# Two batches of chunk 1 transposed by DMA, and chunk 2's first attention products moved into the next stage

## The chip, the cores and the metric

The kernel runs on one core of a Trainium2 chip. The metric is the time of one execution in microseconds (us), as the device measures it; the median of several runs counts. The profiles are those of single executions. Engines are named as in the profile: PE is TensorE (PEld its weight loads), DVE is VectorE, ACT is ScalarE, POOL is GpSimd, SP is SyncE, which only issues DMAs here.

## The reference

Retention (a linear attention with decay), then a feed-forward layer with a tanh GELU. The inputs q, k, v have 4 batches, 8 heads, 768 steps and 64 dimensions; x has 3072 tokens of 512.

```python
gamma = 1.0 - 2.0 ** (-5.0 - np.arange(H))
for t in range(S):
    state = gamma[None, :, None, None] * state + np.einsum('bhd,bhe->bhde', k[:, :, t], v[:, :, t])
    y[:, :, t] = scale * np.einsum('bhd,bhde->bhe', q[:, :, t], state)
x = y.transpose(0, 2, 1, 3).reshape(B * S, H * D)
h = x @ w_in                  # 512 -> 2048
g = 0.5 * h * (1.0 + np.tanh(c * (h + 0.044715 * h * h * h)))
out = g @ w_out               # 2048 -> 512
```

Everything is given and returned in float32.

## The kernel before

**Chunks and stages.** The 768 steps are cut into 6 chunks of 128. A chunk has all 4 batches, so 512 tokens. For each chunk `c` and batch `b` the attention is done in parts: q and k are cast to f16 (`prep1`, on ACT from chunk 1 on; they lie together in a tile `qk`), v is scaled by decays and cast (`prep1` on POOL); q and k are transposed into `qkT`; `mm_A` makes the products of k and q within the chunk on PE, in two PSUM banks of the tag "att" (it has four), and `ev_A` masks them into `a_sb` on DVE; `mm_yc` (what the state from earlier chunks gives) and `mm_yi` (what this chunk gives) are added up in one bank, which `ev_Y` turns into the f16 activations `xT` on DVE; `mm_s` and `ev_S` bring the state `st` up to date. Heads go in pairs, `NHP` = 4.

**Transposes.** There are two ways. `mm_T` and `ev_T` (chunks 0 and 1): 8 PE transposes of a batch into an "att" bank and a copy out of it on DVE or ACT. `dma_T` (from chunk 2 on): one DMA transpose from `qk` to `qkT`, issued on SP's queue, where it waits for the casts of q and k.

**Feed-forward.** M1 of a chunk: `x @ w_in` into "h" banks (two of them), then GELU on ACT into `g`. For chunk 1 M1 has 16 units of 8 matmuls of 256 tokens (`moe1_two`): units 0 to 7 take batches 0 and 1, units 8 to 15 batches 2 and 3. W of a chunk (the change's own words call it M2): `g @ w_out` by a scheme with 7 products instead of 8, each over 8 row pairs `fp` and two halves `a` of tokens, in the banks "o" (two of them). It uses sums of `g` (`g_sums`, results `s_g[1]` to `s_g[4]`, four operations in the order 1 to 4; on POOL for chunk 1, in four calls) and sums of the weights. `units_w(c)` gives W as 14 units, product by product, two halves each: units 0 and 1 take product 0, units 2 and 3 product 1, units 4 and 5 product 2, which reads `s_g[2]`, and so on. Products 0, 2 and 3 are followed by copies on ACT (`s_p`, `s_u`, `s_q`), the others by additions on DVE, and two stores of a chunk go out on POOL's queue. W of chunk 0 is its own list of 15 units (`units_0`, lines 520 to 607), with copies `s_p` (after unit 6), `s_u` (after unit 8) and `s_q` (after unit 9), in which the last product P4 makes units 13 and 14.

**What sets the order.** The schedule is written out by hand. `run(units, after)` calls the units in turn and, after unit `i`, the functions listed in `after[i]`. Each engine carries out its instructions in just this order, and waits where an operand isn't ready or a buffer isn't free. The same goes for SP's queue: a load or a `dma_T` that waits holds up all that stand behind it. The 'ld' buffers hold two chunks of q, k and v in f32.

**Around the change.** The list at line 742 runs W of chunk 0 with chunk 1's attention in between: `preps(1, b)` casts q and k on ACT and v on POOL, `att_T(b)` transposes, `att_1A(b)` is `mm_A` and `ev_A`, `mm_Y` is `mm_yc` and `mm_yi`. The list at line 761 runs M1 of chunk 1; here the rest of chunk 1's attention stands (batches 2 and 3), the casts and transposes of chunk 2 (`prep_qk(2, b)` after units 6, 8, 10 and 12), and after unit 14 the first `mm_A` of chunk 2, of batches 0 and 1, by `att_AY`. The list at line 783 runs W of chunk 1, with chunk 2's attention: `att_AY(2, (0, 1), "h", 2, (2, 3), AC)` makes y of batches 0 and 1 and `mm_A` of batches 2 and 3. The loads of chunk 1 stand on SP at lines 728 to 730, all those of chunk 2 at once behind them (line 731), those of chunk 3 after `prep_qk(2, 3)`.

Of the kernel before, what the change touches and what calls it, by code (L numbers as in the profile page):

```python
# [16 lines left out]
def kernel(  # L17
# [10 lines left out]
    B, H, S, Dh = q.shape  # L28
# [31 lines left out]
    att = ctx.enter_context(tc.tile_pool(name="att", bufs=4))  # L60
# [23 lines left out]
    def load1(eng, nm, c, b):  # L84
        eng.dma_start(
            out=ld_tile(nm, c, b),
            in_=srcs[nm][b, :, c * C:(c + 1) * C, :].rearrange("h p d -> p h d"),
        )
# [60 lines left out]
    def prep1(eng, nm, c, b):  # L149
        if nm == "v":  # L150
            t = pre.tile([128, H, Dh], F16, tag="v16", bufs=2 * B, name="v16")
        else:
            if (c, b) not in qk16:
                qk16[c, b] = pre.tile([128, 2, H, Dh], F16, tag="qk16", bufs=2 * B, name="qk16")
            t = qk16[c, b][:, "qk".index(nm)]
        src = ld_tile(nm, c, b)
        if (nm == "v") == (c < 1):
            copy_on(eng, t, src)
        else:
            col = OQ if nm == "q" else OK  # L160
            eng.tensor_tensor(  # L161
                out=t,
                in0=src,
                in1=cst[:, col:col + H].unsqueeze(2).broadcast_to([128, H, Dh]),
                op=ALU.mult,
            )
        h16[nm, c, b] = t
# [30 lines left out]
    def dma_T(c, b):  # L198

        nc.sync.dma_start_transpose(  # L200
            out=qkT_tile(c, b).rearrange("p i hp t -> p (i hp) t"),
            in_=qk16.pop((c, b)).rearrange("p i h d -> p (i h d)"),
        )
# [411 lines left out]
    VE, AC, PO, SY = nc.vector, nc.scalar, nc.gpsimd, nc.sync  # L615
# [91 lines left out]
    def prep_qk(c, b):  # L707
        prep1(AC, "q", c, b)
        prep1(AC, "k", c, b)
        if c > 1:  # L710
            dma_T(c, b)

    def preps(c, b):
        prep_qk(c, b)
        prep1(PO, "v", c, b)
# [5 lines left out]
    def loads(c, *what):  # L721
        for nm, b in what:
            load1(SY, nm, c, int(b))
# [4 lines left out]
    loads(1, "q0", "k0", "q1", "k1", "v0", "q2", "k2", "v1", "q3", "k3")  # L728
    load_dec()
    loads(1, "v2", "v3")  # L730
    for nm in ("qk", "v"):
        loads(2, *[x + str(b) for b in range(B) for x in nm])

    def att_1A(b):
        mm_A(1, b)
# [2 lines left out]
    def mm_Y(b, tag):  # L738
# [6 lines left out]
            0: [(w_sums, 2), (g_sums, VE, 0, 6, 8)],  # L745
            1: [(w_sums, 3)],
            3: [(preps, 1, 0)],
            5: [(att_T, 0), (preps, 1, 1)],
            7: [(att_1A, 0)],
            8: [(att_T, 1)],  # L750
            9: [(preps, 1, 2)],
            10: [(att_1A, 1)],
            11: [(mm_Y, 0, "h"), (att_T, 2, AC), (ev_Y, 1, 0)],
            12: [(mm_Y, 1, "att"), (ev_Y, 1, 1), (mm_s, 1, (0,)), (preps, 1, 3)],
            13: [(att_1A, 2), (ev_S, 1, (0,))],
            14: [(att_S, 1, 1)],
        },
    )


    run(
# [3 lines left out]
            for fp in range(NF // 2)  # L765
        ],
        {
            0: [(att_T, 3)],
            1: [(mm_Y, 2, "o"), (ev_Y, 1, 2)],
            2: [(att_1A, 3)],  # L770
            3: [(att_S, 1, 2), (g_sums, PO, 1, 0, 4, 0, 1)],
            5: [(mm_Y, 3, "o"), (ev_Y, 1, 3)],
            6: [(att_S, 1, 3), (prep_qk, 2, 0)],
            7: [(g_sums, PO, 1, 4, 8, 0, 1)],
            8: [(prep_qk, 2, 1)],
            10: [(prep_qk, 2, 2)],
            11: [(g_sums, PO, 1, 0, 4, 1, 2)],
            12: [(prep_qk, 2, 3), (load, 3)],
            14: [(att_AY, 1, (), "o", 2, (0, 1), None), (prep1, PO, "v", 2, 0), (prep1, PO, "v", 2, 1)],
            15: [(g_sums, PO, 1, 4, 8, 1, 2), (prep1, PO, "v", 2, 2), (prep1, PO, "v", 2, 3)],  # L780
        },
    )
    run(
        units_w(1),
        {
            4: [(att_AY, 2, (0, 1), "h", 2, (2, 3), AC)],
            6: [(prep_qk, 3, 0)],
            7: [(att_S, 2, 0, 1)],
            8: [(prep_qk, 3, 1)],
            9: [(att_AY, 2, (2, 3), "h", 2, (), AC), (att_S, 2, 2, 3)],  # L790
            10: [(prep1, PO, "v", 3, b) for b in range(B)],
            11: [(prep_qk, 3, 2)],
            13: [(prep_qk, 3, 3)],
        },
# [54 lines left out]
```

## Time and profile before

| | |
|---|---|
| Time of 6 runs, median | 208.9 us (208.4 to 209.17) |
| Time of the profiled execution | 209.07 us |
| Its span, first to last instruction | 207.3 us |
| PE busy | 197.8 us, 95% of the span |
| ACT, POOL, DVE busy | 102.2, 111.3 and 91.5 us |
| W of chunk 0 on PE | from 34.2 to 51.4 us |
| M1 of chunk 1 on PE | from 51.4 to 70.2 us |
| W of chunk 1 on PE | from 70.2 to 86.2 us |

The busy time of an engine is a share of the whole span; how close an engine is to being the limit is read from single stretches. The chain is the work that ended last, followed back from the end from each instruction to what released it. In the views of groups and in the timeline a line gives the start, the length, the engine, the line of the code, the operation, what it writes and reads, and in brackets how long the engine had been idle and what ended that. A line can be that of a helper: line 145 is every copy or cast on ACT through `copy_on`, line 390 every sum through `tt`, line 459 the matmuls of W from chunk 1 on, line 351 those of M1, line 210 is `mm_A`, line 190 `mm_T`, line 200 `dma_T`, line 85 every load. "SPq" is SP's queue; the length of a DMA there is the time for which it holds up the queue, not the time to its landing.

### The profile page before, as it was taken

To read this page: it belongs to the slowest core of one execution; us is meant where nothing else is said; L and a number is where in the kernel's file an instruction comes from. 1 tells how busy PE (TensorE), PEld (TensorE's weight loads), DVE (VectorE), ACT (ScalarE), POOL (GpSimd) and SP (SyncE) were. 2 spreads that over 40 slices of the span, in tenths; PEclk is the share of its full clock that TensorE was granted. 3 is DMA by queue.
4 is the path that set the end of the run, shared out by engine and by line. 5 is a ranking of instruction groups with operands and counts; after the bars stand their busy time and mean duration, and the time that the engine had idled before them with its cause. 6 is when DMAs were issued, how large, how long until landed. Compare 5 with 4: busy or idle time off the path is not lost.

```text
span 207.3 us, 4685 instructions
## 1 busy us (share of the span) xinstructions
PE 197.8 (95%) x1948; PEld 136.0 (66%) x1948; DVE 91.5 (44%) x198; ACT 102.2 (49%) x181; POOL 111.3 (54%) x112
## 2 busy tenths in 40 slices
PE   5789999999999999999999999999999999999993
PEld 1447746877787888644688744678644788544882
DVE  3436389578740448400466400366301374144421
ACT  2365565545369517366445266545366411466321
POOL 0578000225188999549998259997269980200000
PEclk9999999999999999999999999999999999999999
DMA  7999999999989799999990999442520000400005
GB/s 166 288 242 217 206 206 218 255 251 222 323 207 211 177 254 233 215 256 250 268 194 23 216 328 261 90 104 47 164 96 0 2 3 5 202 0 0 3 9 193
DMA packets 98613, 34.23 MB, mean 165 GB/s; under 512 B 92320, under 2 KB 96800, under 8 KB 98592
## 3 DMA queue, kind: packets, MB, share of 16 engines
q1 hardware_dynamic: 86400, 22.40, 49.7%
q0 software_dynamic: 5664, 9.44, 19.0%
q10 hardware_dynamic: 6528, 2.10, 4.0%
q8 instruction: 15, 0.25, 0.5%
q14 instruction: 6, 0.05, 0.1%
HBM read 27.63 MB, written 6.29 MB: 164 GB/s over the span
## 4 chain that ended last, share of the span: by engine, by line
PE 89%; ACT 6%; DMA 2%; POOL 1%; issue 0%; SPq 0%; DVE 0%; POOLq 0%
PE h_ps L351 37%; PE o_ps L459 30%; PE a_ps L210 4%; PE y_ps L247 3%; PE o_ps L530 3%; PE y_ps L234 3%; PE o_ps L563 3%; ACT g L367 2%; PE qkT_ps L190 2%; DMA k<-in_k_dram 2%; ACT qk L145 2%; PE spin_ps L121 2%; PE s_ps L271 2%; ACT qkT L145 1%; POOL qk L161 1%
## 5 line engine op out<-in xcount | busy, mean ns | idle before, releaser
L351 PE MATMUL h_ps<-xT,w_in 128*128 128x512 f16 (+2 forms) x488 | 87.6, 334 | 1.4 <-ACT g L367 1.1
L367 ACT ACTIVATE g<-h_ps 128x512 f16<-128x512 f32 (+1 forms) x98 | 57.1, 588 | 31.9 <-PE h_ps L351 31.9
L351 PEld LDWEIGHTS <-w_in 128*128 128x128 f16 x488 | 45.4, 98 | 38.4 <-issue 3.7
L223 DVE TENSOR_TENSOR a_sb<-a_ps,mask 128x512 f16<-128x512 f32 x48 | 30.1, 683 | 53.2 <-PE a_ps L210 53.1
L390 POOL TENSOR_TENSOR s_g<-g 128x512 f16<-128x512 f16 x32 | 36.9, 1153 | 13.0 <-ACT g L367 13.0
L459 PEld LDWEIGHTS <-s_g 128*128 128x128 f16 x320 | 30.2, 98 | 4.4
L161 POOL TENSOR_TENSOR v<-v,cst 128x512 f16<-128x512 f32 x20 | 20.4, 1045 | 15.9 <-DMA v<-in_v_dram 15.9
L459 PE MATMUL o_ps<-t_w,s_g 128*128 128x256 f16 x240 | 27.8, 273 | 0.0
L459 PEld LDWEIGHTS <-g 128*128 128x128 f16 x240 | 23.5, 98 | 3.6
L390 POOL TENSOR_TENSOR s_g<-s_g,g 128x512 f16<-128x512 f16 x16 | 18.5, 1154 | 1.3
L390 POOL TENSOR_TENSOR s_g<-g,s_g 128x512 f16<-128x512 f16 x16 | 18.5, 1155 | 0.0
L459 PE MATMUL o_ps<-w_out,g 128*128 128x256 f16 x160 | 18.3, 273 | 0.0
L263 DVE TENSOR_TENSOR xT<-y_ps,dec 128x512 f16<-128x512 f32 x20 | 13.1, 688 | 7.0 <-PE y_ps L247 6.9
L492 POOL DMA_DIRECT2D out_dram<-o_sb x8 | 5.9, 739 | 15.9 <-DVE o_sb L390 13.2
L488 ACT COPY o_sb<-o_ps 128x512 f32<-128x512 f32 (+1 forms) x5 | 2.7, 543 | 22.1 <-PE o_ps L459 22.1
L145 ACT CAST qk<-q 128x512 f16<-128x512 f32 x20 | 12.4, 618 | 1.6 <-DMA q<-in_q_dram 1.6
L145 ACT CAST qk<-k 128x512 f16<-128x512 f32 x20 | 12.4, 619 | 0.9 <-DMA k<-in_k_dram 0.9
L390 DVE TENSOR_TENSOR s_g<-g 128x512 f16<-128x512 f16 x16 | 6.7, 421 | 12.6 <-ACT g L367 12.6
L482 ACT COPY s_u<-o_ps 128x512 f32<-128x512 f32 (+1 forms) x6 | 3.1, 515 | 17.3 <-PE o_ps L459 12.1
L390 DVE TENSOR_TENSOR o_sb<-o_ps,s_p 128x512 f32<-128x512 f32 (+1 forms) x7 | 4.3, 615 | 15.4 <-ACT qk L145 8.0
L288 DVE SCALAR_TENSOR_TENSOR st<-st,cst,s_ps 128x128 f16<-128x128 f16 (+1 forms) x40 | 10.0, 314 | 0.5 <-PE s_ps L271 0.5
L459 PE MATMUL o_ps<-w_out,s_g 128*128 128x256 f16 x80 | 9.6, 273 | 0.0
(59 smaller groups left out, 169.1 us busy)
## 6 DMA issues: line engine op xcount, KB each, us to landing
k<-in_k_dram SPq DMA_DIRECT2D x22, 256.0 KB, 4.4
q<-in_q_dram SPq DMA_DIRECT2D x22, 256.0 KB, 4.4
v<-in_v_dram SPq DMA_DIRECT2D x22, 256.0 KB, 4.7
out_dram<-o_sb POOLq DMA_DIRECT2D x10, 512.0 KB, 4.1
w_in<-in_moe_w_in_dram POOLq DMA_DIRECT2D x4, 512.0 KB, 8.4
w_out<-in_moe_w_out_dram POOLq DMA_DIRECT2D x4, 512.0 KB, 13.2
q<-in_q_dram ACTq DMA_DIRECT2D x2, 256.0 KB, 3.6
v<-in_v_dram ACTq DMA_DIRECT2D x2, 256.0 KB, 5.0
```

The lines of the kernel that those rows point to most:

```text
L145: eng.copy(out=out, in_=in_)
L161: eng.tensor_tensor(out=t, in0=src, in1=cst[:, col:col + H].unsqueeze(2).broadcast_to([128, H, Dh]), op=ALU.mult,)
L210: nc.tensor.matmul(out=ps[j][:, hp], lhsT=t[j * 64:(j + 1) * 64, 1, hp], rhs=t[j * 64:(j + 1) * 64, 0, hp], start=True, stop=True,)
L223: nc.vector.tensor_tensor(out=s, in0=ps[j], in1=mask[:, j], op=ALU.mult)
L234: nc.tensor.matmul(out=y_ps[sl, hp], lhsT=st[sl, b, hp], rhs=qkT[c, b][sl, 0, hp], start=(hp == 0), stop=False, skip_group_check=True,)
L247: nc.tensor.matmul(out=y_ps[j * 64:(j + 1) * 64, hp], lhsT=h16["v", c, b][:, 2 * hp + j], rhs=a_sb[c, b, j][:, hp], start=(c == 0), stop=True,
L263: nc.vector.tensor_tensor(out=x, in0=ps, in1=dec, op=ALU.mult)
L288: nc.vector.scalar_tensor_tensor(out=t[:, :, hp], in0=t[:, :, hp], scalar=cst[:, OG + hp:OG + hp + 1], in1=s_ps[:, :, hp], op0=ALU.mult, o ...
L351: nc.tensor.matmul(out=out, lhsT=w_in_sb[wi][:, kc, wr * 128:(wr + 1) * 128], rhs=xT[c][:, kc, t0:t1], start=(kc == 0), stop=(kc == NHP - ...
L367: nc.scalar.activation(out=out, in_=in_, func=AF.Gelu_apprx_tanh, scale=1.0)
L390: eng.tensor_tensor(out=out, in0=in0, in1=in1, op=op)
L459: nc.tensor.matmul(out=po, lhsT=lhs(c, lk, fp, a), rhs=rhs(rk, fp), start=(new and fp == 0 and (last or a == 0)), stop=(stop and fp == NP ...
```

## The change

- Batches 2 and 3 of chunk 1 are transposed by `dma_T` like all later chunks; their `att_T` calls are taken out. `preps(1, 1)` moves from unit 5 to unit 6 of `units_0`, behind the copy `s_p`; `preps(1, 2)` from unit 9 to 8; `preps(1, 3)` from unit 12 to 10. `att_1A(2)` moves from unit 13 to 14, `att_1A(3)` from unit 2 to 1 of M1, `mm_Y(2)` from unit 1 to 2.
- The loads of chunk 2's q and k are issued on SP behind the two new transposes. Those of its v follow, two each, behind the first and the second transpose of chunk 2.
- The casts and transposes of chunk 2 come one unit of M1 later: after units 7, 9, 11 and 13. The loads of chunk 3 stay behind the last of them.
- `mm_A` and `ev_A` of chunk 2's batches 0 and 1 move from unit 14 of M1 to unit 1 of W. The attention steps that stood after units 4 and 9 of W come after units 5 and 10; the prep of chunk 3's v comes after unit 9 instead of 10.

```diff
@@ prep_qk
-        if c > 1:
+        if (c, b) > (1, 1):
             dma_T(c, b)
@@ loads
     loads(1, "v2", "v3")
-    for nm in ("qk", "v"):
-        loads(2, *[x + str(b) for b in range(B) for x in nm])
@@ run(units_0(), ...)
             3: [(preps, 1, 0)],
-            5: [(att_T, 0), (preps, 1, 1)],
+            5: [(att_T, 0)],
+            6: [(preps, 1, 1)],
             7: [(att_1A, 0)],
-            8: [(att_T, 1)],
-            9: [(preps, 1, 2)],
-            10: [(att_1A, 1)],
-            11: [(mm_Y, 0, "h"), (att_T, 2, AC), (ev_Y, 1, 0)],
-            12: [(mm_Y, 1, "att"), (ev_Y, 1, 1), (mm_s, 1, (0,)), (preps, 1, 3)],
-            13: [(att_1A, 2), (ev_S, 1, (0,))],
-            14: [(att_S, 1, 1)],
+            8: [(att_T, 1), (preps, 1, 2)],
+            10: [(att_1A, 1), (preps, 1, 3)],
+            11: [(mm_Y, 0, "h"), (ev_Y, 1, 0)],
+            12: [(mm_Y, 1, "att"), (ev_Y, 1, 1), (mm_s, 1, (0,))],
+            13: [(ev_S, 1, (0,))],
+            14: [(att_1A, 2), (att_S, 1, 1)],
         },
     )
+    loads(2, "q0", "k0", "q1", "k1", "q2", "k2", "q3", "k3")
@@ run of M1 of chunk 1
-            0: [(att_T, 3)],
-            1: [(mm_Y, 2, "o"), (ev_Y, 1, 2)],
-            2: [(att_1A, 3)],
+            1: [(att_1A, 3)],
+            2: [(mm_Y, 2, "o"), (ev_Y, 1, 2)],
             3: [(att_S, 1, 2), (g_sums, PO, 1, 0, 4, 0, 1)],
             5: [(mm_Y, 3, "o"), (ev_Y, 1, 3)],
-            6: [(att_S, 1, 3), (prep_qk, 2, 0)],
-            7: [(g_sums, PO, 1, 4, 8, 0, 1)],
-            8: [(prep_qk, 2, 1)],
-            10: [(prep_qk, 2, 2)],
-            11: [(g_sums, PO, 1, 0, 4, 1, 2)],
-            12: [(prep_qk, 2, 3), (load, 3)],
-            14: [(att_AY, 1, (), "o", 2, (0, 1), None), (prep1, PO, "v", 2, 0), (prep1, PO, "v", 2, 1)],
+            6: [(att_S, 1, 3)],
+            7: [(g_sums, PO, 1, 4, 8, 0, 1), (prep_qk, 2, 0), (loads, 2, "v0", "v1")],
+            9: [(prep_qk, 2, 1), (loads, 2, "v2", "v3")],
+            11: [(g_sums, PO, 1, 0, 4, 1, 2), (prep_qk, 2, 2)],
+            13: [(prep_qk, 2, 3), (load, 3)],
+            14: [(prep1, PO, "v", 2, 0), (prep1, PO, "v", 2, 1)],
             15: [(g_sums, PO, 1, 4, 8, 1, 2), (prep1, PO, "v", 2, 2), (prep1, PO, "v", 2, 3)],
@@ run(units_w(1), ...)
-            4: [(att_AY, 2, (0, 1), "h", 2, (2, 3), AC)],
+            1: [(att_AY, 1, (), "att", 2, (0, 1), None)],
+            5: [(att_AY, 2, (0, 1), "h", 2, (2, 3), AC)],
             6: [(prep_qk, 3, 0)],
             7: [(att_S, 2, 0, 1)],
             8: [(prep_qk, 3, 1)],
-            9: [(att_AY, 2, (2, 3), "h", 2, (), AC), (att_S, 2, 2, 3)],
-            10: [(prep1, PO, "v", 3, b) for b in range(B)],
+            10: [(att_AY, 2, (2, 3), "h", 2, (), AC), (att_S, 2, 2, 3)],
+            9: [(prep1, PO, "v", 3, b) for b in range(B)],
```

## The prediction

> **What bounds the kernel now.** The page first:
>
> ```profile
> span 207.3 us, 4685 instructions
> PE 197.8 (95%) x1948; PEld 136.0 (66%) x1948; DVE 91.5 (44%) x198; ACT 102.2 (49%) x181; POOL 111.3 (54%) x112
> PE 89%; ACT 6%; DMA 2%; POOL 1%; issue 0%; SPq 0%; DVE 0%; POOLq 0%
> ```
>
> TensorE runs 95% of the span and is 89% of the chain, so a TensorE instruction saved is time saved, and any new wait of TensorE is time lost. TensorE's waits, whole run, show how little it waits today (the rest of the list lies before 20 us):
>
> ```profile
> PE h_ps L351 <- ACT g L367: 1.1, 4, 0.5
> PE o_ps L563 <- ACT s_p L541: 0.2, 1, 0.2
> ```
>
> Next the chain around the last units of chunk 0's output stage and the first of chunk 1's M1, which gives TensorE's prices:
>
> ```profile
> 47.12 0.55 PE qkT_ps L190 x8
> 47.67 0.44 PE o_ps L530 x4
> ...
> 48.92 0.98 PE o_ps L563 x8
> 49.90 0.33 PE a_ps L210 x8
> 50.23 0.98 PE o_ps L563 x8
> 51.21 0.24 PE s_ps L271 x8
> 51.45 0.98 PE h_ps L351 x8
> 52.43 0.45 PE qkT_ps L190 x8
> ```
>
> Columns: start, length, what. A transposed batch is 0.45 us, 0.55 where TensorE comes from half-array matmuls; a full-array group of 8 is 0.98 after these, 0.87 in a row. So a change of shape costs 0.11.
>
> GpSimd through the turn from M1 to W of chunk 1:
>
> ```profile
> 71.87 2.05 POOL L161 TENSOR_TENSOR v<-v,cst 128x512 f16<-128x512 f32 x2
> 73.87 1.16 POOL L390 TENSOR_TENSOR s_g<-g 128x512 f16<-128x512 f16 x1
> 75.11 1.16 POOL L390 TENSOR_TENSOR s_g<-s_g,g 128x512 f16<-128x512 f16 x1
> ```
>
> It works without a break from 62.73 to 83.5 us. The second sum of its last group ends at 76.27. TensorE needs it in W's unit 5 (product 2, half a = 1), from the fifth of eight row pairs on:
>
> ```profile
> 75.67 0.64 PE L247 MATMUL y_ps<-a_sb,v 128*64 128x128 f16 x16
> 76.24 2.79 PE L459 MATMUL o_ps<-t_w,s_g 128*128 128x256 f16 x24
> ```
>
> The chain has this restart at 76.30; 0.11 and four matmuls (0.44) later is 76.85. The sums have 0.58 us in hand, no more.
>
> SyncE's queue and the landing of its last load of chunk 1 (issued at 43.94) and of its first transpose (62.18):
>
> ```profile
> 43.26 2.67 SPq L85 DMA_DIRECT2D v<-in_v_dram  x2
> 46.03 1.25 SPq L85 DMA_DIRECT2D q<-in_q_dram  x1
> ...
> 62.18 7.44 SPq L200 DMA_TRANSPOSE qkT<-qk  x4
> 69.67 0.57 SPq L85 DMA_DIRECT2D q<-in_q_dram  x1
> ```
>
> ```profile
> DMA to landing us min/median/max: 5.2/5.2/5.2
> ```
>
> ```profile
> DMA to landing us min/median/max: 5.0/5.0/5.0
> ```
>
> [...] the load issued at 61.11 lands 5.3 later (66.4), the transpose at 67.2, and at 81.8 us the same (85.9, 86.8): 0.85 behind. [...] the burst's second transpose (issued 64.55, 3.8 to land) comes 1.1 after the first, as loads come 0.9 apart. [...] DVE's add into s_u waits 0.36 us for ScalarE's copy s_q of the same bank.
>
> **The change part by part, for TensorE.**
>
> Up to 47.12 nothing is removed. Casts (1,1) behind s_p: s_p runs 40.39 to 40.98 for TensorE's sake, ScalarE having been idle for 0.59; so nothing is gained. The casts then end at 42.1, transposing starts at 43.37: hidden, with 1.3 in hand.
>
> Casts (1,2) now precede the copy s_q: it moves from 44.29 to 45.0, DVE's add behind it from 44.91 to 45.6, and all of DVE's queue by 0.7 (ev_A of batch 1, two adds, two ev_Y). The add frees the bank of y (batch 0) at 46.3, which TensorE takes at 46.44; ev_A ends at 47.5, needed at 48.0; ev_Y (batch 1) ends at 50.0, needed at 50.8. Hidden, by 0.1 to 0.8.
>
> Removed: transposing of batch 2, 0.44 (of its 0.55, 0.11 goes to its successor), and of batch 3, 0.45. mm_A of batch 2 moves from between the two halves of P4 to behind them, beside mm_s: one change of shape less into P4 (0.11) and one into s (0.12). Sum 1.12. The two copies out of PSUM (ScalarE 1.01, DVE 0.68) go too, but TensorE didn't wait for them.
>
> New wait 1: mm_A(1,2), at 50.3, needs a transfer. The casts end at 45.1, SyncE is free at 45.93, so it issues at about 46.1, in the place of the load at 46.03. By the load ahead (43.94 + 5.2 = 49.15) and 0.85 it lands at 50.0: hidden by 0.3. Lower bound 2.7, the shortest landing in the trace (48.8); upper bound 5.0 (51.1, a loss of 0.8). I take 50.0, loss 0. Batch 3 lands about 1.1 later, its mm_A is at 52.6. Behind mm_A(1,2) stand mm_s and all of M1.
>
> M1: M1's unit 3 ends 1.12 earlier, unit 7 too (before 61.65, now 60.53). Then casts of chunk 2 come after units 7, 9, 11, 13 rather than 6, 8, 10, 12. ScalarE's cycle of two GELUs and two casts is 2.07 us (62.05, 64.15, 66.17, 68.26 start the pairs of GELUs), TensorE's two units 1.74, so TensorE waits in either kernel. Following bank by bank (unit n needs the GELU of n-2): units 8 to 15 take 8.17 now. Before, from 61.65 to 70.25, they took 8.60 with 0.66 of mm_A(2,0..1) and its change of shape, 7.94 without: mm_A and the mm_s had filled waits. Loss 0.23. M1 ends at 60.53 + 8.17 = 68.70, before 70.25: ahead by 1.55.
>
> W: mm_A(2,0..1) now stands after unit 1, 0.55 + 0.11 = 0.66 added.
>
> New wait 2: the attention group of 1.68 (0.56 + 0.55 + 0.57) goes from before unit 5 to behind it. TensorE wants the fifth pair at 68.70 + 1.75 + 0.66 + 2.62 + 0.44 = 74.17. GpSimd's chain starts from GELUs: its second group at 62.73 came 1.08 after unit 7's end because casts stood ahead of that GELU; now 0.79 after, 61.32. Its length to the second sum's end stays 76.27 - 62.73 = 13.54: 74.86, with release 74.91. Loss 0.74. Behind it stand unit 5's other matmuls, then attention.
>
> Sum at W's end: -1.12 + 0.23 - 0.66 (that left M1) + 0.66 + 0.74 = -0.15. Checked from the other side: TensorE wants the fifth pair at 76.85 now and gets it at 74.91, 1.94 earlier, but then still has the attention group and a change of shape to do, 1.68 + 0.11: again 0.15 ahead. So what sets the end here is GpSimd's chain, and a TensorE delay of up to 0.7 between M1's unit 7 and W's unit 5 would cost nothing.
>
> SyncE's queue: the eight q, k loads of chunk 2 go behind two transposes; they took 11 us in landing (50.1 to 61.1), now some 53 to 64, and their casts start at 61.3 with the first pair, 67.5 the last: hidden by 3. Four v loads (4.10) and four transposes (5.0 to 7.4) interleave from 62.4 on, so chunk 3's loads start at 70.6 to 73.9, I take 72, before 69.67. mm_A(2,1) at 71.0 needs the transpose issued at 65.5 and landed by 69.3; v0, v1 land by 68.2, wanted by GpSimd at 70.5. GpSimd's prep of chunk 3's last v waits for its landing (before 86.03) and two stores follow; then 2.55 idle until chunk 2's sums. A delay of 2.3 fits in.
>
> The profiled execution took 209.07 with span 207.3; it goes to 208.9 (span 207.15). The six runs' median is 208.9, 0.17 under it: forecast 208.8.
>
> **Rivals.** (1) The transpose of batch 2 is late, slower. Place: mm_A(1,2). For: at 62.2 and 81.8 the first transpose of a burst took 5.0. Against: there the load ahead had 4.2 still to go, here 3.05. Every us beyond 50.3 counts whole (GELUs, and so sums, move along). At 5.0: +0.8 on the forecast, 209.6; with the 0.15 ahead it decides (slower by over 0.42) from 50.9 on. (2) Wait 2 isn't paid (sums run quicker, or TensorE comes later than I count for a reason that costs nothing): -0.89, 208.0. Against: GpSimd's pace is even. (3) Chunk 3's loads slip by over 2.65 (2.55, plus 0.25 that chunk 2's sums have, less 0.15): W of chunk 2 then waits, us for us: at 73.9 (4.2 late) +1.55, 210.3. Against: at 72, where I put them, it costs nothing. (4) That the change doesn't do what it says: if batches 2 and 3 were still transposed on TensorE, 0.89 of the saving would be missing; the condition in prep_qk and the removed calls speak against it, so it has no chance of its own.
>
> **How the numbers follow.** What this kernel's measurement can tell from no change is about 0.2%, 0.42 us. The forecast case 0.46 (0.36 same, 0.06 faster, 0.04 slower; own range 208.4 to 209.2); rival 1 0.24 (0.23 slower, the rest same at its edge); rival 2 0.18, faster; rival 3 0.12, slower. Faster 0.24, same 0.37, slower 0.39. The range, 208.1 to 210.0, cuts half of rival 2's far side and rival 3's tail.
>
> **What would show it.** Right: 48 transposing matmuls at L190 (64 before); 18 DMA transposes (16); no wait at L210 near 50.3; a wait of TensorE for POOL s_g of 0.5 to 0.9 near 74; SyncE's chunk 3 loads from about 72. Wrong: TensorE's L210 waiting for DMA, no wait for s_g, or TensorE waiting for POOL in chunk 2's W.

## The result and the profile after

The changed kernel takes 210.42 us in the median of 28 runs (the kernel before 209.07 in 63 runs): a ratio of 1.0061 with a 95% interval of 1.005 to 1.0072, so 1.05 to 1.5 us slower. The forecast was 208.8, range 208.1 to 210.0: too low, and on the wrong side. Two of the 28 runs fell in a slower state of the chip and are left out of the ratio. The profiled execution took 209.72, only 0.65 more than that of before; the reason for this gap is part of the answer.

The page of the changed kernel, span and chain by engine:

```profile
span 208.0 us, 4649 instructions
PE 61%; DMA 17%; POOL 11%; SPq 8%; issue 1%; ACT 1%; DVE 0%; POOLq 0%
```

The chain was TensorE for 89% before; it now runs over DMAs, SyncE's queue and GpSimd for a third of the span. TensorE's busy time fell by 1.1 us with the 16 transposing matmuls, and the time didn't follow. Its waits (whole run, what is new or longer):

```profile
PE h_ps L351 <- ACT g L367: 1.9, 5, 0.8
...
PE o_ps L459 <- POOL s_g L390: 0.6, 1, 0.6
PE a_ps L210 <- DMA qkT<-qk: 0.3, 1, 0.3
```

The chain at the end of W of chunk 0 (start, length, what), to be read against the lines of before from 47.12 us on:

```profile
41.50 4.35 DMA k<-in_k_dram
45.85 4.30 DMA qkT<-qk
...
50.20 0.40 PE a_ps L210 x8
```

`mm_A` of batch 2 starts when the transpose lands, at 50.15. In TensorE's timeline:

```profile
50.20 0.40 PE L210 MATMUL a_ps<-qkT 64*128 64x128 f16 x8 [0.25 <-DMA qkT<-qk]
```

The turn from M1 to W of chunk 1, GpSimd's timeline and then TensorE's:

```profile
73.73 1.15 POOL L390 TENSOR_TENSOR s_g<-s_g,g 128x512 f16<-128x512 f16 x1
```

```profile
74.94 0.61 PE L459 MATMUL o_ps<-t_w,s_g 128*128 128x256 f16 x4 [0.59 <-POOL s_g L390]
```

That is the wait for the sums, and it is where the forecast put it (74.91). The chain at the start of chunk 2's M1:

```profile
82.89 4.73 DMA k<-in_k_dram
...
87.64 0.04 ACT qk L145
...
88.17 0.60 ACT g L367
```

The load of chunk 3's last k lands at 87.62 (before at 83.80). Its cast stands on ScalarE ahead of chunk 2's first GELU, so TensorE waits 0.79 us there instead of 0.48. Before, then after:

```profile
88.44 9.72 PE L351 MATMUL h_ps<-xT,w_in 128*128 128x512 f16 x44 [0.48 <-ACT g L367]
```

```profile
88.81 9.72 PE L351 MATMUL h_ps<-xT,w_in 128*128 128x512 f16 x44 [0.79 <-ACT g L367]
```

Where the 0.66 us of the span went, by stage, from the stages' starts in TensorE's two timelines, before and then after (W of chunk 0, W of chunk 1, M1 of chunk 2, W of chunk 2; M1 of chunk 1 lies between the first two):

```profile
34.06 1.91 PE L530 MATMUL o_ps<-w_out,g 128*128 128x256 f16 x16
...
70.09 3.66 PE L459 MATMUL o_ps<-w_out,g 128*128 128x256 f16 x32
...
86.07 1.89 PE L351 MATMUL h_ps<-xT,w_in 128*128 128x512 f16 x8
...
101.25 3.66 PE L459 MATMUL o_ps<-w_out,g 128*128 128x256 f16 x32
```

```profile
33.69 1.91 PE L530 MATMUL o_ps<-w_out,g 128*128 128x256 f16 x16
...
68.72 1.91 PE L459 MATMUL o_ps<-w_out,g 128*128 128x256 f16 x16
...
86.13 1.89 PE L351 MATMUL h_ps<-xT,w_in 128*128 128x512 f16 x8
...
101.61 3.66 PE L459 MATMUL o_ps<-w_out,g 128*128 128x256 f16 x32
```

| Stage | before, us | after, us | difference | forecast |
|---|---|---|---|---|
| up to W of chunk 0 | 34.06 | 33.69 | -0.37 | 0 |
| W of chunk 0 and M1 of chunk 1 | 36.03 | 35.03 | -1.00 | -1.55 |
| W of chunk 1 | 15.98 | 17.41 | +1.43 | +1.40 |
| M1 of chunk 2 | 15.18 | 15.48 | +0.30 | 0 |
| the rest, to TensorE's last matmul | 102.79 | 102.76 | -0.03 | 0 |
| from there to the span's end | 3.26 | 3.59 | +0.33 | 0 |

The first row is chance: nothing before W of chunk 0 was changed, and over the profiled executions of all kernels here W of chunk 0 starts between 32.80 and 34.65. The difference in the last row lies behind the last instruction of every compute engine.

### The profile page after: what moved, and what is told of

The parts are those of the page before. It is cut to its first block, busy times and chain, and to the rows that moved or that the text cites. A ratio compares the mean times of both kernels' runs of the same rounds, so it can differ in the third digit from the quotient of the medians.

```text
span 208.0 us, 4649 instructions
## 1 busy us (share of the span) xinstructions
PE 196.7 (95%) x1932; PEld 135.0 (65%) x1932; DVE 90.0 (43%) x197; ACT 101.5 (49%) x180; POOL 111.6 (54%) x112
## 3 DMA queue, kind: packets, MB, share of 16 engines
q1 hardware_dynamic: 88512, 22.92, 50.3%
## 4 chain that ended last, share of the span: by engine, by line
PE 61%; DMA 17%; POOL 11%; SPq 8%; issue 1%; ACT 1%; DVE 0%; POOLq 0%
PE h_ps L351 30%; PE o_ps L459 24%; DMA k<-in_k_dram 8%; DMA w_out<-in_moe_w_out_dram 7%; SPq L85 7%; POOL s_g L390 7%; DMA qkT<-qk 2%; PE y_ps L247 2%; PE y_ps L234 2%; PE a_ps L210 2%; POOL qk L161 2%; POOL w_in L332 1%; POOL v L161 1%; PE s_ps L271 1%; POOL w_out L341 1%
```

## The experiments

Ratios are against the kernel before on the same chip, with the 95% interval; 0.1% is 0.21 us. The runs lie on several chips and the changed kernel was measured in one group of runs only, so where two ratios are subtracted, it is taken for granted that the chip makes no difference to them. "The changed kernel" is the base of each diff unless the kernel before is named. Waits are TensorE's, in the run's own profiled execution, which is one execution and not the median one.

The theory from these profiles: the loss is made of three waits: that for the DMA transpose of chunk 1's batch 2 (T from here on), that for the sums in W, and that for the last k of chunk 3 (the late k; it shows as a wait for a GELU). The rivals: that moving chunk 2's attention makes the whole loss, or that each wait taken away only uncovers another.

**One suspect at a time.** x1_a_later moves `mm_A` of batch 2 behind M1's first unit:

```diff
-            14: [(att_1A, 2), (att_S, 1, 1)],
+            14: [(att_S, 1, 1)],
@@ M1 of chunk 1
+            0: [(att_1A, 2)],
```

> The changed kernel with mm_A of chunk 1's batch 2 after unit 0 of M1 instead of before it, so that TensorE doesn't wait for the DMA transpose (0.33 us in the changed kernel's profile). Theory S (the start of M1 of chunk 2 is set by the last load of k of chunk 3, through the cast and the GELU behind it; what is won before is lost there): no wait at L210 for DMA, but +0.9 to +1.3 us on the kernel before, as the changed kernel itself. Theory I (each wait counts by itself): 0.3 to 0.6 us below the changed kernel, so +0.7 to +1.0.

Measured: 1.0038 [1.0019, 1.0058]. No wait for T; the sums' wait is still 0.60. So T's wait is about 0.5 us of the loss by the medians, more than the 0.25 of the one profile; the two intervals just overlap.

x2_sums_dve puts the last of chunk 1's groups of sums on VectorE (`g_sums, VE, 1, 4, 8, 1, 2` for `PO`), to take the wait for them away:

> The changed kernel with the last group of sums of g of chunk 1 on VectorE instead of GpSimd, so that TensorE doesn't wait for them in unit 5 of W (0.59 us in the profile). Theory S: the wait is gone, TensorE comes to M1 of chunk 2 about 0.6 us earlier and waits there as much longer, 1.3 to 1.5 us instead of 0.79; +0.9 to +1.3 us on the kernel before. Theory I: 0.6 below the changed kernel, +0.6 to +0.8.

Measured: 1.0091 [1.0056, 1.0127], worse. The wait for the sums went, but VectorE's timeline has

```profile
69.90 1.27 DVE L390 TENSOR_TENSOR s_g<-g 128x512 f16<-128x512 f16 x1 [8.98 <-ACT g L367]
```

for an operation that takes 0.42 on average where VectorE makes all sums of a chunk (chunks 0 and 5; GpSimd has no sums or preps during them in the trace of before). The four sums took 1.15 to 1.27 us, close to the 1.16 of GpSimd's sum and the 1.2 of each of its four preps of v that ran beside them. GpSimd's 20 preps of v took 1.080 on average here, 1.041 in the changed kernel, so both engines were slower side by side; by what, was not shown. VectorE's masking `ev_A` then came late, and TensorE waited 0.61 for it. This run doesn't price the sums' wait.

x3_casts_dve puts the casts of chunk 3's batch 3 on VectorE, so that they don't stand ahead of a GELU:

```diff
-            13: [(prep_qk, 3, 3)],
+            13: [(prep1, VE, "q", 3, 3), (prep1, VE, "k", 3, 3), (dma_T, 3, 3)],
```

> The changed kernel with the casts of q and k of chunk 3's batch 3 on VectorE, which is idle there, so that no GELU of M1 of chunk 2 stands behind a cast that waits for its load. Theory S: the wait of 0.79 us is gone, and with it what varies from run to run: +0.0 to +0.5 us on the kernel before. Theory I: 0.8 below the changed kernel, +0.3 to +0.5. A third theory (the loss of typical runs lies elsewhere, in transfers that the profile of one run doesn't show): still +0.8 or more.

Measured: 1.0062 [1.003, 1.0094], as the changed kernel. The GELU wait is gone and another has come, in W of chunk 2. GpSimd's timeline, then TensorE's:

```profile
89.56 1.05 POOL L161 TENSOR_TENSOR v<-v,cst 128x512 f16<-128x512 f32 x1 [3.06 <-PE h_ps L351]
...
92.04 1.17 POOL L390 TENSOR_TENSOR s_g<-g 128x512 f16<-128x512 f16 x1
```

```profile
108.22 2.14 PE L459 MATMUL o_ps<-t_w,s_g 128*128 128x256 f16 x18 [0.85 <-POOL s_g L390]
```

GpSimd's prep of the last v comes late as well, two stores and chunk 2's sums follow it without a pause, and W of chunk 2 waits for them. That is the prediction's third rival, uncovered as soon as the GELUs are no longer late themselves. T's wait was 1.52 in this execution, which had started early (32.94).

x5_v_early loads chunk 2's v directly behind its k instead of between the transposes:

> The changed kernel with the loads of chunk 2's v issued directly behind those of its q and k, ahead of the transposes of chunk 2, where SyncE's queue is idle from 60.4 to 62.3 us. Theory L (chunk 3's loads, which start at 72.6 instead of 69.7, hold up either the GELU at M1 of chunk 2 or, through GpSimd, the sums in W of chunk 2): chunk 3's loads start at 70 to 70.5, the GELU's wait is back at 0.5 us, no wait for sums in W of chunk 2; 0.3 to 0.7 us below the changed kernel, +0.5 to +0.9 on the kernel before. Theory N (the late loads cost nothing in typical runs): as the changed kernel, +1.2.

Measured: 1.0043 [1.0025, 1.0061]. Chunk 3's loads started at 72.39, hardly earlier than in the changed kernel (72.61), its last k landed at 88.80, and the GELU wait was 1.67. So moving the v loads there doesn't make chunk 3 earlier. The median is where the theory of the late loads had put it, but neither the earlier loads nor the shorter GELU wait that it forecast came: the number fits by luck.

x6_att_back puts the second attention group of chunk 2 back to unit 4 of W, as it was before (`4: [(att_AY, 2, (0, 1), ...)]` for `5:`):

> The changed kernel with the attention group of W of chunk 1 back after unit 4, ahead of unit 5. Theory G (GpSimd's sums bind unit 5): TensorE's wait of 0.59 us for s_g is gone, but the loads of chunk 3 are as late as before, so TensorE waits longer for the GELU at M1 of chunk 2 (1.2 to 1.4): +0.9 to +1.3 on the kernel before. If the waits count each by itself: +0.6 to +0.7.

Measured: 1.0103 [1.0059, 1.0147]. The wait for the sums is gone and nothing is gained: its execution lost 1.39 to T and 1.50 to the last k (landed 88.34). These are six runs only.

x9_qk_first loads all q and k of chunk 3 ahead of its v:

> The changed kernel with the loads of chunk 3 in another order: q and k of all four batches first, then v. Theory L (the DMA engines are full from 33 us on; two more transposes push chunk 3's loads back by 2 to 3 us or more, the last k then lands behind the time when ScalarE wants to cast it, and the GELU behind it waits): the last k lands some 2.7 us earlier, the GELU's wait is back at 0.5 us, and 0.3 to 1.0 us of the loss go: +0.3 to +0.9 on the kernel before. The rival (the loss of typical runs is the wait for the transpose and for the sums alone): as the changed kernel, +1.2.

Measured: 1.0093 [1.0059, 1.0126]. The GELU wait is back at 0.48, and W of chunk 2 waits 0.81 for the sums, since now the v are late: the same load time, paid elsewhere. This execution started earliest (32.80) and met the longest wait for T, in TensorE's timeline:

```profile
51.25 0.61 PE L210 MATMUL a_ps<-qkT 64*128 64x128 f16 x8 [2.02 <-DMA qkT<-qk]
51.79 0.43 PE L271 MATMUL s_ps<-v,qk 128*64 128x64 f16 x8
52.15 3.14 PE L351 MATMUL h_ps<-xT,w_in 128*128 128x256 f16 x16
```

The last line is 16 matmuls, which take 1.92 elsewhere: the granted clock was 0.5 from 51.3 to 54.7 us. The DMA engines' busy share was 0.91 to 1.08 in the four stretches 33 to 50, 50 to 62, 62 to 75 and 75 to 88 us of the changed kernel, and 0.89 to 1.01 in those of this run. This profile took 213.04 us, 1.4 above the run's median.

**Several together.** x4_all is x1, x2 and x3 in one; x7_three is x1, x5 and x6; x8_four adds x3 to x7; x10_fix3 is x1, x6 and x9.

> The three edits together. Both S and I: all three waits gone, the 1.1 us of TensorE work that the change saves show, and the 0.48 us that the kernel before waited at the same GELU go too, less 0.2 to 0.3 us of waits for ScalarE in M1: -1.0 to -1.5 us on the kernel before. Third theory: -0.5 or worse.

> The changed kernel with mm_A of batch 2 after unit 0 of M1, the v loads early and the attention group back after unit 4. If the three waits (transpose 0.3 to 0.7, sums 0.6, late loads 0.3 to 0.9) are all that turned the saving of 1.1 us of TensorE work into a loss: no wait for the transpose, none for sums, 0.5 for the GELU as in the kernel before; -0.7 to -0.9 us (1.1 less 0.23 for ScalarE in M1 and 0.1 of a change of shape). If something else costs: 0 or above.

> The same with the casts of q and k of chunk 3's batch 3 on VectorE as well, which takes away the wait of 0.5 us for the GELU that the kernel before has too: -1.2 to -1.4 us on the kernel before; as x7_three or worse if VectorE's casts or what follows from them hold up something else.

> The changed kernel with mm_A of batch 2 after unit 0 of M1, the attention group of W back after unit 4, and chunk 3's q and k loaded before its v. Theory L with the two other waits: no wait for the transpose of batch 2, none for sums, 0.5 us for the GELU: -0.3 to -0.9 us on the kernel before. If DMA traffic finds another place to hold TensorE up (the transposes of chunk 2, GpSimd's v of chunk 3): 0 or above.

Measured: x4_all 1.003 [1.001, 1.005], x7_three 1.0072 [1.0037, 1.0106], x8_four 1.0094 [1.0071, 1.0118], x10_fix3 1.009 [1.0054, 1.0127]. None reached the kernel before. In x4_all the slow sums on VectorE cost 0.61 at `mm_A`. In x7_three and x8_four the v loads ahead of chunk 2's transposes made these late (1.76 + 0.66 and 1.22 + 0.66 of waiting at `mm_A` of chunk 2), with half the clock for some 3.4 us after it (granted clock 0.5 from 73.9 to 77.3 us in x7_three); the profile of x7_three is 2.0 us above its median, so these waits needn't be typical. In x10_fix3 T landed only at 51.46, 0.84 too late even for the later `mm_A`, and W of chunk 2 waited 1.66 for its sums. So far the second rival fitted better than the theory: a wait taken away came up again behind it.

**The two halves of the change.** w_only is the kernel before with only the move of chunk 2's attention into W (M1's and W's lists of the change, without its DMA transposes):

> The kernel before with only the move of chunk 2's attention into W of chunk 1 (casts and transposes of chunk 2 one unit of M1 later, mm_A of batches 0 and 1 after unit 1 of W, the attention groups after units 5 and 10); all of chunk 1's batches are transposed on TensorE, loads as before. By the prediction's own steps: ScalarE in M1 +0.23, a wait for the sums of about 0.7 in unit 5 of W, chunk 3's loads about 1 us later at no cost: +0.7 to +1.1. If the move is free and the loss comes from the transposes' traffic: 0.0 to +0.3.

t_only is the other half: the two transposes by DMA, with their casts and loads, and chunk 2's attention where it was (`14: [(att_AY, 1, (), "o", 2, (0, 1), None), ...]` in M1, the next group at unit 4 of W):

> The transposes of chunk 1's batches 2 and 3 by DMA, with the moved loads and casts, but chunk 2's attention left where it was (first products in M1, the next group after unit 4 of W). My theory: the wait for the transpose (0 to 2 us, 0.9 on average) and the wait for the last k of chunk 3 (0.3 to 1.2 us over the kernel before) stay, the wait for the sums in W is gone or under 0.3: 0.3 to 0.9 us slower than the kernel before. Rival, that the move of the attention makes the whole loss: faster than before by about 0.9.

Measured: w_only 1.0017 [1, 1.0035], t_only 1.0042 [1.0019, 1.0064]; together 0.59%, and the whole change has 0.61%. So neither half alone is the loss; the transposes' median is the larger, but the intervals overlap. That the two add up so well is in part luck, as t_only has a wait that the whole change hasn't. In t_only TensorE's timeline shows two waits for transposes, and none for sums:

```profile
50.66 0.40 PE L210 MATMUL a_ps<-qkT 64*128 64x128 f16 x8 [0.87 <-DMA qkT<-qk]
...
69.21 0.40 PE L210 MATMUL a_ps<-qkT 64*128 64x128 f16 x8 [0.76 <-DMA qkT<-qk]
```

The second is chunk 2's: the loads behind the new transposes push the old ones back, past an `mm_A` that stayed in M1; of what was expected the number came, and of the two waits only the one for T. In w_only the move costs less (0.36 us) than the 0.7 to 1.1 expected from the prediction's steps, whose lower end its interval just reaches; the sums' wait is 0.60, as in the whole change. Chunk 3's last k landed at 85.43 in w_only and 85.38 in t_only, 1.6 later than before and without a loss (GELU wait 0.48 in both); only both together bring it to 87.62, where it costs. The traffic of two more transposes alone, with TensorE's work as before, has no measurement.

b_sp is the kernel before with the casts of batch 1 behind `s_p` (`6: [(preps, 1, 1)]` for `5:`), the edit that the prediction gave nothing:

> The kernel before with one edit of the change alone: the casts of chunk 1's batch 1 behind the copy s_p. My prediction gave it nothing, since TensorE did not wait there in the profile of before. After the runs, my theory is that executions which start W of chunk 0 early lose their lead there, waiting for s_p behind casts that wait for a load: 0.1 to 0.5 us faster in the median. Rival: no difference (within 0.1).

Measured: 1.0016 [1.0002, 1.003]: no gain, my theory fell. An early execution does lose its lead there without the edit: w_only, started at 32.80, waits 1.29 for `s_p`, b_sp, started at 32.93, only 0.24. But b_sp then waits 0.48 for a transpose of chunk 2 at 68.39. So in these two executions a lead that passes one transfer is lost, in part, at the next.

**The cause of the late transpose.** x12_v_behind issues chunk 1's last two v loads behind the two new transposes instead of ahead of them:

```diff
     load_dec()
-    loads(1, "v2", "v3")
...
-            10: [(att_1A, 1), (preps, 1, 3)],
+            10: [(att_1A, 1), (prep_qk, 1, 3), (loads, 1, "v2", "v3")],
```

(batch 2's `preps` likewise, and the v preps of both after unit 14)

> The changed kernel with chunk 1's last two v loads issued behind the two new DMA transposes instead of ahead of them. If the failed step is that the transpose lands behind the loads ahead of it in the DMA queue: it lands at about 48.8 us instead of 50.2 to 51.4, TensorE's wait at mm_A of batch 2 is gone in every execution, and the median is 0.3 to 0.9 us below the changed kernel's (0.4 to 0.9 above the kernel before). If the landing has another cause: no change, 1.2 above the kernel before. The later v of batches 2 and 3 may cost a wait at mm_Y of batch 2, up to 0.5.

Measured: 1.0038 [1.0016, 1.0059], 0.23% or 0.5 us below the changed kernel's ratio (the intervals overlap). T landed at 48.34, and nobody waited for it though this execution started at 32.86. So the loads ahead make T's landing. What was won went into the last k (landed 88.06), in TensorE's timeline

```profile
89.25 9.72 PE L351 MATMUL h_ps<-xT,w_in 128*128 128x512 f16 x44 [2.33 <-ACT g L367]
```

x13_full takes all three waits away at once: x12, the second attention group back after unit 4, the casts of x3, and GpSimd's prep of chunk 3's last v behind the two stores.

```diff
-            5: [(att_AY, 2, (0, 1), "h", 2, (2, 3), AC)],
+            4: [(att_AY, 2, (0, 1), "h", 2, (2, 3), AC)],
-            9: [(prep1, PO, "v", 3, b) for b in range(B)],
+            9: [(prep1, PO, "v", 3, b) for b in range(3)],
-            13: [(prep_qk, 3, 3)],
+            13: [(prep1, VE, "q", 3, 3), (prep1, VE, "k", 3, 3), (dma_T, 3, 3), (prep1, PO, "v", 3, 3)],
```

> As the run with the v loads behind, and chunk 2's second attention group back after unit 4 of W, the casts of chunk 3's batch 3 on VectorE, and GpSimd's prep of that batch's v behind the two stores. If wait for the sums, late last k of chunk 3 and late v prep are all that the change costs behind the first transpose: all three waits gone, 0.6 to 1.2 us below the kernel before. If one wait only takes the place of another (the DMA engines being full): level with the kernel before or slower.

Measured: 0.9979 [0.9963, 0.9995], faster than the kernel before. TensorE has no wait of its profiled execution left that the kernel before doesn't have, beyond the forecast two in M1 (0.46 and 0.20); the last k landed at 88.11, as late as ever:

```profile
86.00 6.27 PE L351 MATMUL h_ps<-xT,w_in 128*128 128x512 f16 x28
```

M1 of chunk 2 runs into it without a stop, for nobody ahead of a GELU or a sum needs that load any more. So the theory of the three waits holds. No set of repairs without x12's came below the kernel before, though not every set was tried. Two limits: the gain of 0.44 us is under the expected 0.6 to 1.2 (the interval reaches 0.77), and the casts on VectorE also take away the 0.48 us for which the kernel before waits at the same GELU. That kernel with this edit alone wasn't measured, so x13_full doesn't show that the change itself, mended, is a gain.

**Behind the last instruction.** All kernels with the two new transposes showed spans that end 2.97 to 2.99 us after the last instruction of a compute engine, the others 2.61 to 2.63. The trace's events after the last store show why: SyncE waits in turn for nine semaphores of DMAs, some 0.06 us apart. In the kernel before the one of the last store is the ninth (over at 206.39); in the changed kernel it is the third (206.70), and six more follow, to 207.07. d2_before adds two DMAs of 128 bytes to the kernel before, in the idle queue during chunk 5; d6_after and d6_full add six to the changed kernel and to x13_full.

```diff
     for c in range(2, NCk):
         n, m = c + 1, c + 2
+        if n == NCk:
+            for _ in range(2):
+                nc.sync.dma_start(out=iden[0:1, 0:64], in_=iden_h.ap()[0:1, 0:64])
```

> The kernel before with two more DMAs of 128 bytes on SyncE's queue after chunk 5's attention, where nothing else is loaded and nobody waits for them. Seen in the traces: SyncE ends every execution by waiting in turn for nine DMA semaphores; in the kernel before the one of the last store is the ninth, in every kernel with the two new transposes the third, with six more waits of 0.06 us behind it, and the span then ends 2.97 to 2.99 us after the last engine instruction instead of 2.61 to 2.63. If this depends only on how many DMAs a program issues: the end is 2.98 us here too and the time 0.36 us above the kernel before. Rival, that the transposes themselves make it: 2.62, no change in time.

> The changed kernel with six such small DMAs. If the place of the last store's semaphore goes round with the count of DMAs, by eight: the end is 2.62 us again and the loss falls by 0.36 us, from 1.3 to about 0.9 above the kernel before. Rival: end 2.98, loss 1.3.

> The changed kernel with the v loads behind the transposes, the second attention group back after unit 4, the casts of chunk 3's batch 3 on VectorE and the last v prep behind the stores (0.35 us below the kernel before as measured), with six such small DMAs. By my theory 0.36 us less: 0.7 us below the kernel before. Rival, that the end is not counted in the time: 0.35 below as without them.

Measured: in the spans as expected: 2.97 for d2_before, 2.62 and 2.60 for d6_after and d6_full, the last store's semaphore third, ninth and ninth. So the count of DMAs makes it, not the transposes. In the times: d6_after 1.0034 [1.0018, 1.005], 0.27% below the changed kernel's ratio; d6_full 0.9959 [0.9938, 0.998], 0.2% below x13_full's; d2_before 1.0002 [0.9985, 1.0019], where 1.0017 was expected, just inside its interval. Two of three medians fit the 0.36 us (0.17%), the third shows nothing of it. Since the time of an execution is 1.76 to 1.80 us over its span in the five profiles concerned (before, after, and these three), and 1.71 to 1.85 in all runs, I hold that it counts; the medians alone don't settle it.

d6_full is the fastest version here: 208.17 us in the median, 0.4 to 1.3 us below the kernel before (its interval). The waits of its profiled execution, two for chunk 2's transposes (0.81 and 0.36) and one for sums (0.54), are those of a late one, 1.2 us above that median.

## Why the prediction was wrong

By its own steps:

- **"Up to 47.12 nothing is removed", casts behind `s_p`: nothing gained.** Right: b_sp shows no gain.
- **Removed, "Sum 1.12".** A little high. M1's unit 7 ends 1.06 earlier (60.48 against 61.54, the line x24 at 59.61 and its last unit); less 0.37 of early start and plus the 0.25 of T's wait, 0.94 are the change's. The change of shape into `mm_s` that was counted as saved (0.12) isn't: `mm_s` takes 0.24 in both kernels.
- **"New wait 1 ... I take 50.0, loss 0": the step that failed.** As a reading of one execution it was good: issued at 45.85, landed at 50.15. But "hidden by 0.3" took TensorE's arrival from a single profile, and a late one (W of chunk 0 from 34.06). Eight profiled executions with this part unaltered (after, t_only, x2, x3, x5, x6, x9 and d6_after) have T landing between 50.15 and 51.21, and waits of 0.25, 0.87, 0.21, 1.52, 0, 1.39, 2.02 and 0.57: 0.85 on average. The landing is tied to the loads ahead, not to TensorE, so who comes early waits: a loss that is nothing in the latest execution and 2 us in the earliest. On average T lands 0.6 after the 50.0 that was taken, and TensorE, which starts W of chunk 0 at 33.51 on average, comes about 0.55 before the 50.3; less the cover of 0.3 this makes the 0.85. The place is rival 1's, and the sign (L210 waiting for DMA) is one that the prediction had named, but rival 1 has only the landing late, which is half of it. It also fits that the median lost more (1.3 us) than the profiled execution (0.65), which met only 0.25 of it and had started 0.37 earlier than the one of before. Without this wait the median is 0.5 us lower in x1, and 0.5 in x12, where part of what was won went to the late k. That T lands behind the loads ahead was right: with two loads fewer ahead, it lands at 48.34 (x12) and 48.46 (x13), about 1.7 or more earlier.
- **M1, "Loss 0.23".** Right: units 8 to 15 took 8.24 (60.48 to 68.72), forecast 8.17.
- **"New wait 2 ... Loss 0.74".** Right in place and mechanism; 0.59 measured in after, d6_after and x9, 0.60 in x1, x3 and w_only. Rival 2 is excluded.
- **"SyncE's queue ... A delay of 2.3 fits in": the second step that failed.** Chunk 3's loads start 2.94 later (72.61, taken as 72), its last k lands 3.82 later. I priced only GpSimd's prep of the last v. The casts of the last k stand on ScalarE ahead of chunk 2's first GELU, and these have no 2.5 us in hand: TensorE waited 0.14 to 1.85 us over the old 0.48 in the changed kernel, x1, x5, x6, x12 and d6_after (in x2, where TensorE came later, no more than 0.48). Rival 3, as written, is what comes next when that is mended (x3, x9, x10).
- **A term that was missing: the end.** "It goes to 208.9 (span 207.15)" took everything behind the last matmul as fixed. It is 0.34 us longer in the trace; no step of the prediction asked what the two DMAs more would do there.

The loss of 1.3 us is what costs leave over savings, so the 0.94 saved (from one pair of profiles) counts too: costs of 2.2 have to be found. The end has 0.34 of them by the trace, and the move of the attention 0.36 by w_only (its two longer waits for GELUs in M1 and the 0.6 for the sums, less its own saving of shape changes). The other 1.5 are T's and the late k's together. In profiles T's wait is 0.85 on average, and the late k 0.31 and 0.14 in the two of this schedule; the 0.4 that is missing is as much as the intervals leave open, and how the 1.5 divides isn't shown. The single repairs can't be added up, since what is won at one wait is partly lost at the next.

Why executions start W of chunk 0 up to 1.9 us apart wasn't tried. The granted clock goes with it in part: in four of the five profiles that start it after 34.0 (x2, x5, x13, d2_before) the page has a mean clock of 0.7 to 0.8 from 5.2 to 10.4 us and of 0.5 to 0.7 from there to 15.6; of the six that start it before 33.0 (x3, x9, x10, x12, w_only, b_sp) only b_sp has less than 0.9 there (0.7 to 0.8, then 0.8 to 0.9). But the kernel before, which starts it at 34.06, has 0.9 or more in both.

## What to carry to other kernels

A transfer that one profile shows as hidden by a few tenths isn't hidden if TensorE's arrival varies by more than that and the landing doesn't vary with it: ask whether the profiled execution is an early or a late one. When DMAs are added to a queue that is busy from end to end, follow the last load behind them to every engine that has it in front of work that is due, not to one of them. Moves that each uncover the next wait have to be tested together: here each single repair showed 0.5 us or nothing, and all of them gained 1.7 us over the changed kernel, of which the 0.48 at the GELU could be had without the change as well (an estimate from the profile of before).

## What was unexpected of the hardware

- **Half the clock after a short wait.** After the wait of 2.02 us in x9 the granted clock was 0.5 for 3.4 us. It cost about 1.6 us: from `mm_A` of batch 2 to the first wait for a GELU in M1 took 14.22 instead of 12.66. The same came after the double waits of x7 (1.76 and 0.66) and x8 (1.22 and 0.66). After 2.33 in x12 the clock stayed at 1.00 (84 to 98 us), and after 1.67 in x5 it is 0.9 or more in every slice of the page from 15.7 us on. So the length of one wait doesn't tell whether the clock falls; what does was not shown.
- **The end of the program moved with its count of DMAs**, by 0.34 to 0.37 us of span, through the place of the last store's semaphore among nine.
- **VectorE's sum of two f16 operands beside GpSimd's preps of v**: 1.15 to 1.27 us instead of 0.42 (x2, x4).
